# B and C of eight pairs loaded by head pair and stretch and turned on VectorE, the state of six pairs packed

## The chip, the cores and the metric

The kernel runs on one core of a Trainium2 chip. The metric is the device time of one execution in microseconds. Below, PE is TensorE (PEld its weight loads), DVE is VectorE, ACT is ScalarE, POOL is GpSimd and SP is SyncE, which here only issues DMAs.

## What is computed

A state-space scan, followed by a gated feed-forward layer without biases. There are 4 batches, 8 heads, 768 tokens, 32 channels a head (D) and 16 state rows (N). Cut to what matters:

```python
log_a = np.log(np.clip(a, 1e-06, 1.0))
for c in range(nc):                       # chunks of 32 tokens
    cum = np.cumsum(la, axis=-1)
    L = np.exp(cum[:, :, :, None] - cum[:, :, None, :]) * causal
    M = np.einsum('bhin,bhjn->bhij', Cc, Bc) * L
    y_intra = np.einsum('bhij,bhjd->bhid', M, xc)
    y_inter = np.einsum('bhin,bhnd->bhid', Cc, state) * np.exp(cum)[:, :, :, None]
    y[:, :, sl] = y_intra + y_inter
    Bx = np.einsum('bhjn,bhjd->bhjnd', Bc, xc) * np.exp(cum[:, :, -1:] - cum)[..., None, None]
    state = np.exp(np.sum(la, axis=-1))[:, :, None, None] * state + np.sum(Bx, axis=2)
x = y.transpose(0, 2, 1, 3).reshape(3072, 256)
out = (np.maximum(x @ w_gate, 0) * (x @ w_val)) @ w_out     # 256 -> 1536 -> 256
```

Inputs and output are float32. The decay from token j to token i is a product of the a between them, so a ratio of prefix products: C can be multiplied by the prefix product of its token, B by its inverse, and no decay is left between the two.

## The kernel before

**Tiling.** The scan works in chunks of 128 tokens, two chunks to a pair: 12 pairs of 256 tokens, three pairs to a batch (PPB). The feed-forward layer works in blocks of 512 tokens (two pairs): for each of 12 slices of the hidden width, gv (or gvp for 256 tokens and two slices) makes gate and val in PSUM, ACT takes the relu of gate (r), DVE multiplies by val (h). outs(b, ts) then multiplies 128 tokens of h by wo (o), ACT evacuates and SP stores.

**A pair of the scan** passes through these steps. load brings x, B and C of 256 tokens (tokens on the partitions; for pairs 4 to 11 a piece of B or C is one head's 16 values, 64 bytes). scale_bc (POOL) multiplies B and C by their decays. cast_x (POOL) makes x bf16. turn (PE, transp) transposes B and C against an identity. tevac copies C (ACT) and multiplies B twice by a 0/1 mask (DVE, for some pairs ACT), giving BT and CT with heads and state rows on the partitions. G makes C.B of each head, four row tiles of 32 partitions beside each other, into four PSUM buffers. gevac moves them to gs with the causal mask: part by DVE with maskUT, part by an ACT copy and a POOL affine_select (causal). astep adds B.x of a chunk to A_ps, all heads against all heads in one matmul of 256 columns, and sevac multiplies by smask, which keeps the blocks of equal heads (Sm, DVE). inter adds C.state to y, Dm (dterm) adds gs.x in sixteen column tiles of 32, and yevac writes yT, the feed-forward layer's input. Pairs 0 to 3 (NWIDE) are loaded two tokens to a partition and use variants (load_wide, sort_b, split_y).

**Decays.** cp is the prefix product of a along half sequences (two scans on DVE); wide_decay, decay and inverse turn it to token order through PE and keep it with its reciprocal (scaleBC).

**PSUM.** Seven buffers are shared by all steps (bank, tag "shared"), the eighth holds A_ps.

**Order.** The order of the work is written out by hand, and in_order at the end pins every engine to it: an engine executes its instructions in program order. Where pair 1 stands, for instance, POOL has weights(6, 9), cast_x(1), the masks of gevac(1, 4), weights(9, NF), and later scale(2). Around f = 8 of block 0, DVE has state(2, 0), gevac(2, 3), h of f = 8, then h of 9, 10 and 11; its neighbours on POOL are scale_bc(3), the load of wo and cast_x(3). From block 2 on a loop runs over the blocks, with the scan's steps set at fixed f.

Of the kernel before, what the change touches and what calls it, by code (L numbers as in the profile page):

```python
# [29 lines left out]
def kernel(  # L30
# [39 lines left out]


    NWIDE = 4
    st = {}

    def load_wide(p, q=nc.sync, hold=False):
        b, c0 = p // PPB, 2 * (p % PPB)
        sl = slice(c0 * 128, (c0 + 2) * 128)
        bcr = raw.tile([128, NH, 2, 2, N], FP32, tag="bcr", name="bcr")
        if hold:
            nc.vector.memset(bcr[0:1, 0, 0, 0, 0:1], 0.0)  # L80
        for src, j in ((B, 0), (C, 1)):
            q.dma_start(
                out=bcr[:, :, j].rearrange("p h r n -> p h (r n)"),
                in_=src[b, :, sl, :].rearrange("h (p r) n -> p h (r n)", r=2))
        st[p] = {"bcr": bcr}

    def load_x(p, hold=False):
# [9 lines left out]
    def load(p, q):  # L97
        b, c0 = p // PPB, 2 * (p % PPB)
        xr = raw.tile([128, 2, NH, D], FP32, tag="xr", name="xr")
        bcr = raw.tile([128, 2, 2, NH, N], FP32, tag="bcr", name="bcr")  # L100
        for i in range(2):
            sl = slice((c0 + i) * 128, (c0 + i + 1) * 128)
            q.dma_start(out=xr[:, i], in_=x[b, :, sl, :].rearrange("h s d -> s h d"))
            for src, j in ((B, 0), (C, 1)):
                q.dma_start(out=bcr[:, i, j],
                            in_=src[b, :, sl, :].rearrange("h s n -> s h n"))
# [22 lines left out]
    zero1 = const.tile([2 * BH, 1], FP32)  # L129
    nc.vector.memset(zero1, 0.0)  # L130
    tmask = const.tile([128, 2], FP32)
    nc.vector.memset(tmask, 0.0)
    smask = const.tile([128, 2, 128], BF16)
    nc.vector.memset(smask, 0.0)
# [4 lines left out]
    for q in range(4):  # L139
        r = slice(32 * q, 32 * q + 32)  # L140
        c = 64 * (q % 2)
        nc.vector.tensor_copy(
            smask[r, q // 2, c:c + 64].rearrange("p (t d) -> p t d", t=2),
            tmask[r].unsqueeze(2).to_broadcast([32, 2, 32]))
    pick = const.tile([2 * BH, 2, BH], FP32)
    pairs = identf.rearrange("p (h w) -> p w h", w=2)
    nc.vector.tensor_copy(pick[:, 1], pairs[:, 1])
# [46 lines left out]
    nc.vector.reciprocal(rmid, cp[:, H - 1:H])  # L194
    nc.vector.tensor_scalar_mul(pick[:, 0], pairs[:, 0], rmid)

    def wide_decay(ps):

        d = bank("wdec", (128, len(ps), 2, 8))
        first = True  # L200
        for k, p in enumerate(ps):
            b, c0 = p // PPB, 2 * (p % PPB)
            for i in range(2):
                w, o = (c0 + i) // HC, ((c0 + i) % HC) * 128
                for r in range(2):
                    nc.tensor.matmul(  # L206
                        out=d[64 * i:64 * i + 64, k, r],
                        lhsT=cp[:, o + r:o + 128:2], rhs=pick[:, w, 8 * b:8 * b + 8],
                        start=first or (k == 0 and r == 0), stop=True,
                        tile_position=(0, 64 * i), skip_group_check=True)  # L210
                first = False
        return d
# [53 lines left out]
    def inverse(b, c0, c1):  # L266
        nc.vector.reciprocal(scaleBC[:, b, c0:c1, 0, :], scaleBC[:, b, c0:c1, 1, :])

    yT = glob.tile([128, 2, T], BF16)
    A_ps = mm.tile([128, 2, 128], FP32, tag="Aps", name="A_ps")  # L270


    def scale(p, eng, ceng):
# [3 lines left out]
    def scale_bc(p, eng):  # L277
        b, c0 = p // PPB, 2 * (p % PPB)
        s = st[p]
        bs = att.tile([128, 4, 128], BF16, tag="bs", name="bs")  # L280
        if p < NWIDE:
            src = s["bcr"].rearrange("s h j r n -> s (j r) h n")
            f = factors[p]
        else:
            src = s["bcr"].rearrange("s i j h n -> s (i j) h n")
            f = scaleBC[:, b, c0:c0 + 2].rearrange("s c j h -> s (c j) h")
        eng.tensor_tensor(  # L287
            out=bs.rearrange("s k (h n) -> s k h n", h=NH), in0=src,
            in1=f.to_broadcast([128, 4, NH, N]), op=ALU.mult)
        if p < NWIDE:  # L290
            s["tin"] = [[bs[:, 2 * j + r] for r in range(2)] for j in range(2)]
            s["sort"] = s["tin"][0]
        else:
            s["tin"] = [[bs[:, 2 * i + j] for i in range(2)] for j in range(2)]
            s["B"] = s["tin"][0]

    def cast_x(p, ceng):
        s = st[p]
# [80 lines left out]
    def G(p):  # L379
        s = st[p]  # L380
        g = [bank("g%d" % q, (128, 2, 2, 128)) for q in range(4)]
        for i in range(2):
# [49 lines left out]
    def sevac(p, i):  # L432
        if 2 * (p % PPB) + i == NC - 1:
            return
        S[2 * p + i + 1] = n = att.tile([128, 2, 128], BF16, tag="Sm", name="Sm", bufs=5)
        nc.vector.tensor_tensor(out=n, in0=A_ps, in1=smask, op=ALU.mult)  # L436

    def state(p, i):
        astep(p, i)
        sevac(p, i)  # L440

    def y_bank(s):
        if "y" not in s:
# [33 lines left out]
    def dterm(p, out, k, i, start):  # L477

        s = st[p]
        for c in range(4):  # L480
            h = 4 * k + c
            nc.tensor.matmul(  # L482
                out=out[32 * c:32 * c + 32], lhsT=s["x"][i][:, h * D:(h + 1) * D],
                rhs=s["gs"][:, h // 2, 2 * i + h % 2], start=start, stop=True,
                tile_position=(0, 32 * c), skip_group_check=True)

    def Dm(p):
# [109 lines left out]
    def section(p, n, s=None):  # L597

        inter(p, 0)
        inter(p, 1)  # L600
        Dm(p)
        if n < NPAIR:
            G(n)
        if s is not None:
# [1 line left out]
        yevac(p, nc.scalar)  # L606
        if n < NPAIR:
            gevac(n)

    def Gs(p):  # L610
        G(p)
        gevac(p)
# [83 lines left out]
    turn(2, True)  # L696
    sort_b(2, False)
    tevac(2, nc.vector, nc.scalar)
    gv(0, 6)
    sort_evac(2)  # L700
    gv(0, 7)
    G(2)
    u = gv(0, 8, False)
    state(2, 0)
    gevac(2, 3)
    gv_evac(*u)
    scale_bc(3, nc.gpsimd)
    weights_out(0, NF)
    cast_x(3, nc.gpsimd)
    gv(0, 9)  # L710
    gv(0, 10)
# [18 lines left out]
    scale(4, nc.gpsimd, nc.gpsimd)  # L730
    gvp(1, 0, 6)
    gvp(1, 0, 8)
    inter(3, 1)
    Dm(3)
    astep(3, 1)
    yevac(3, nc.scalar)
    sevac(3, 1)
    scale(5, nc.gpsimd, nc.gpsimd)
    gvp(1, 0, 10)
    for f in range(0, 10, 2):  # L740
        gvp(1, 1, f)
    turn(4)
    tevac(4, nc.vector, nc.scalar)
    gvp(1, 1, 10)
    outs(0, 0)
    state(4, 0)
    Gs(4)
    outs(0, 1)
    state(4, 1)
    inverse(2, 0, 6)  # L750
    load(7, nc.sync)
    outs(0, 2)
    turn(5)
    tevac(5, nc.vector, nc.scalar)
    scale(6, nc.gpsimd, nc.gpsimd)
    outs(0, 3)
    load(8, nc.sync)
# [1 line left out]
    state(5, 0)  # L759
    outs(1, 0)  # L760
    inverse(3, 0, 6)
    turn(6)
    tevac(6, nc.vector, nc.scalar)
    outs(1, 1)
    outs(1, 2)
    section(5, 6)
# [2 lines left out]
    for b in range(2, NBLK):  # L769
        P, Q, R = 2 * b + 2, 2 * b + 3, 2 * b + 4  # L770
        more = P < NPAIR
        for n in (P + 3, P + 4):
            if n < NPAIR:
                load(n, nc.sync)
        fst[b] = ffn.tile([128, NF, 512], BF16, tag="h", name="h")
        for f in range(NF):
# [2 lines left out]
                continue  # L779
            if f == 0:  # L780
                scale(Q, nc.gpsimd, nc.gpsimd)
            if f == 1:
                state(P - 1, 1)
            if f == 3:
                turn(Q)
                tevac(Q, nc.vector, nc.scalar)
            if f == 4 and R < NPAIR:
                scale(R, nc.gpsimd, nc.gpsimd)
            if f == 6:
                state(P, 0)  # L790
# [45 lines left out]
```

## Time and profile before

| | |
|---|---|
| time, median of the runs | 127.63 us |
| the profiled execution: time, span | 127.66 us, 126.0 us |
| PE busy | 120.2 us, 95% of the span |
| DVE, ACT, POOL busy | 86.5, 76.9, 42.0 us |
| share of PE on the chain that ended last | 91% |
| DMA moved | 12.10 MB in 74,287 packets, 67,040 of them under 512 B |
| TensorE clock granted | 1.0 throughout |

The profile is one execution on the chip. Busy time is summed over an engine's instructions. The chain is followed back from the last instruction, at each step to what released it. A row of a timeline gives start, duration, engine, line, operation, output and inputs, count, and in brackets the idle time before it and who ended it. A row of groups gives count, busy time, mean duration in ns, then the idle time before.

### The profile page before, as it was taken

To read this page: it belongs to the slowest core of one execution; us is meant where nothing else is said; L and a number is where in the kernel's file an instruction comes from. 1 tells how busy PE (TensorE), PEld (TensorE's weight loads), DVE (VectorE), ACT (ScalarE), POOL (GpSimd) and SP (SyncE) were. 2 spreads that over 40 slices of the span, in tenths; PEclk is the share of its full clock that TensorE was granted. 3 is DMA by queue.
4 is the path that set the end of the run, shared out by engine and by line. 5 is a ranking of instruction groups with operands and counts; after the bars stand their busy time and mean duration, and the time that the engine had idled before them with its cause. 6 is when DMAs were issued, how large, how long until landed. Compare 5 with 4: busy or idle time off the path is not lost.

```text
span 126.0 us, 3223 instructions
## 1 busy us (share of the span) xinstructions
PE 120.2 (95%) x1224; PEld 82.0 (65%) x1224; DVE 86.5 (69%) x174; ACT 76.9 (61%) x153; POOL 42.0 (33%) x72
## 2 busy tenths in 40 slices
PE   6899899999999999999999999999999999999990
PEld 4578585578898988744578654588544588444770
DVE  6876978888987665579692689691798870578410
ACT  5066747979774463877863776945676634776310
POOL 7988661765405361444030660030800030000000
PEclk9999999999999999999999999999999999999999
DMA  2999999999979679989983386002200003100022
GB/s 54 197 194 180 170 153 184 140 106 165 168 90 118 106 111 158 139 181 137 119 93 78 103 104 72 5 3 83 86 5 0 0 0 128 44 0 0 0 97 70
DMA packets 74287, 12.10 MB, mean 96 GB/s; under 512 B 67040, under 2 KB 74272, under 8 KB 74272
## 3 DMA queue, kind: packets, MB, share of 16 engines
q1 hardware_dynamic: 67632, 9.02, 46.2%
q0 software_dynamic: 4272, 2.36, 14.5%
q10 hardware_dynamic: 2368, 0.52, 2.0%
q8 instruction: 9, 0.15, 0.4%
q14 instruction: 6, 0.05, 0.1%
HBM read 11.11 MB, written 3.15 MB: 113 GB/s over the span
## 4 chain that ended last, share of the span: by engine, by line
PE 91%; DMA 2%; DVE 2%; POOL 1%; ACT 1%; issue 0%
PE o L565 25%; PE gate L515 19%; PE val L518 19%; PE gate L539 6%; PE val L539 6%; PE g L386 3%; PE y L482 3%; DMA a_sb<-in_a_dram 2%; PE A_ps L428 2%; PE tp L333 2%; PE y L472 2%; POOL gs L394 1%; DVE cp L189 1%; PE w L161 1%; PE wdec L206 1%; PE dec L253 1%
## 5 line engine op out<-in xcount | busy, mean ns | idle before, releaser
L527 DVE TENSOR_TENSOR h<-r,val 128x512 bf16<-128x512 bf16 x54 | 36.5, 685 | 14.4 <-ACT r L526 13.0
L526 ACT ACTIVATE r<-gate 128x512 bf16<-128x512 f32 x54 | 31.9, 599 | 10.7 <-PE gate L515 9.1
L565 PE MATMUL o<-wo,h 128*128 128x256 bf16 x288 | 34.1, 273 | 0.0
L515 PE MATMUL gate<-yT,wg 128*128 128x512 bf16 x108 | 32.1, 379 | 0.0
L518 PE MATMUL val<-yT,wv 128*128 128x512 bf16 x108 | 32.1, 379 | 0.0
L565 PEld LDWEIGHTS <-h 128*128 128x128 bf16 x288 | 27.6, 98 | 3.9
L394 POOL TENSOR_SCALAR_AFFINE_SELECT gs<-gs 128x512 bf16<-128x512 bf16 (+1 forms) x26 | 13.5, 546 | 47.1 <-ACT gs L411 47.1
L418 DVE TENSOR_TENSOR gs<-g,maskUT 128x512 bf16<-128x512 f32 (+1 forms) x32 | 17.5, 599 | 10.0 <-issue 8.2
L518 PEld LDWEIGHTS <-wv 128*128 128x128 bf16 x108 | 10.6, 98 | 12.7
L515 PEld LDWEIGHTS <-wg 128*128 128x128 bf16 x108 | 10.2, 98 | 9.6
L554 DVE TENSOR_TENSOR h<-r,val 128x512 bf16<-128x512 bf16 x18 | 12.1, 684 | 2.1 <-ACT r L547 1.2
L411 ACT CAST gs<-g 128x512 bf16<-128x512 f32 (+1 forms) x26 | 11.8, 513 | 2.5 <-PE g L386 2.5
L547 ACT ACTIVATE r<-gate 128x512 bf16<-128x512 f32 x18 | 10.7, 602 | 4.2 <-PE gate L539 3.7
L287 POOL TENSOR_TENSOR bs<-bcr,scaleBC 128x512 bf16<-128x512 f32 x8 | 8.5, 1058 | 9.2 <-DMA bcr<-in_C_dram 5.6
L539 PE MATMUL gate<-yT,wg 128*128 128x256 bf16 x72 | 10.8, 273 | 0.0
L539 PE MATMUL val<-yT,wv 128*128 128x256 bf16 x72 | 10.8, 273 | 0.0
L579 ACT COPY ob<-o 128x256 f32<-128x256 f32 x11 | 4.1, 372 | 9.3 <-PE o L565 8.9
L436 DVE TENSOR_TENSOR Sm<-A_ps,smask 128x256 bf16<-128x256 f32 x20 | 8.3, 417 | 1.9 <-PE A_ps L428 1.7
L584 ACT COPY ob<-o 128x512 f32<-128x512 f32 x6 | 3.5, 585 | 8.0 <-PE o L565 8.0
L539 PEld LDWEIGHTS <-wv 128*128 128x128 bf16 x72 | 7.0, 98 | 0.8
L301 POOL CAST xb<-xr 128x512 bf16<-128x512 f32 x11 | 6.7, 609 | 2.6 <-DMA xr<-in_x_dram 2.6
L503 ACT CAST yT<-y 128x512 bf16<-128x512 f32 x10 | 5.9, 585 | 2.5 <-PE y L482 2.4
(86 smaller groups left out, 105.1 us busy)
## 6 DMA issues: line engine op xcount, KB each, us to landing
xr<-in_x_dram SPq DMA_DIRECT2D x24, 128.0 KB, 3.4
out_dram<-ob SPq DMA_DIRECT2D x6, 256.0 KB, 2.6
out_dram<-ob SPq DMA_DIRECT2D x10, 128.0 KB, 1.9
bcr<-in_B_dram SPq DMA_DIRECT2D x16, 64.0 KB, 3.2
bcr<-in_C_dram SPq DMA_DIRECT2D x16, 64.0 KB, 3.0
wo<-in_moe_w_out_dram POOLq DMA_DIRECT2D x1, 768.0 KB, 8.8
bcr<-in_B_dram SPq DMA_DIRECT2D x3, 128.0 KB, 4.8
wg<-in_moe_w_gate_dram POOLq DMA_DIRECT2D x3, 128.0 KB, 4.8
```

Source lines behind the costliest of these rows:

```text
L287: eng.tensor_tensor(out=bs.rearrange("s k (h n) -> s k h n", h=NH), in0=src, in1=f.to_broadcast([128, 4, NH, N]), op=ALU.mult)
L394: nc.gpsimd.affine_select(out=dst, in_=dst, pattern=[[0, n], [1, 128]], compare_op=ALU.is_ge, fill=0.0, base=0, channel_multiplier=-1)
L411: nc.scalar.copy(out=d[:, q, h], in_=g[q][:, h])
L418: nc.vector.tensor_tensor(out=d[:, q, h], in0=g[q][:, h], in1=m[:, h], op=ALU.mult)
L515: nc.tensor.matmul(out=g, lhsT=wg[:, k, fs], rhs=yT[:, k, tk], start=(k == 0), stop=(k == 1))
L518: nc.tensor.matmul(out=v, lhsT=wv[:, k, fs], rhs=yT[:, k, tk], start=(k == 0), stop=(k == 1))
L526: nc.scalar.activation(r, g, AF.Relu)
L527: nc.vector.tensor_tensor(out=fst[b][:, f], in0=r, in1=v, op=ALU.mult)
L539: nc.tensor.matmul(out=o[:, j], lhsT=w[:, k, fs], rhs=yT[:, k, tk], start=(k == 0), stop=(k == 1), skip_group_check=True)
L547: nc.scalar.activation(r, g, AF.Relu)
L554: nc.vector.tensor_tensor(out=fst[b][:, f:f + 2, u * 256:(u + 1) * 256], in0=r, in1=v, op=ALU.mult)
L565: nc.tensor.matmul(out=o[:, ts % 2], lhsT=fst[b][:, f, ts * 128:(ts + 1) * 128], rhs=wo[:, f], start=(f == 0), stop=(f == NF - 1), skip_gr ...
```

## The change

For batches 1 to 3 (except pair 3's own wide load) B and C are also loaded a whole batch at a time (load_seq): partition 32q + j holds stretch j of 24 tokens of the heads q and q + 4, so a contiguous piece is 24 x 16 values, 1,536 bytes. Their decays are made in the same layout: a is loaded so (load_a), one DVE scan gives the products inside all stretches, the stretch totals are turned, scanned and turned back (seq_decay) and multiplied in on POOL. seq_scale (POOL, 768 elements a partition) applies them; seq_turn (DVE) transposes 32x32 blocks, which gives heads and state rows on the partitions and the batch's 768 tokens along them; seq_mask (POOL) makes the two masked copies of B. G takes its slices from there. The transposes on PE, their evacuation, and the token-order load of C go for pairs 4 to 11; B is still loaded in token order too, for the state. Heads are paired q with q + 4 from batch 1 on.

For pairs 6 to 11 (NRUN on) the state is made by arun in the section that precedes the pair: column tiles of 32, only for blocks of paired heads, into a part of the A_ps buffer, with both states of a pair evacuated by one DVE product against a wider smask.

In the order: smask_seq (eight small POOL copies) and three memsets stand behind cast_x(1); load_a behind load_x(2); load_seq(1) ahead of load(4) and load_seq(2) ahead of load(6); the local scan behind gv(0, 6), seq_decay behind h of f = 8; seq_scale(1, "B") ahead of G(3) and its masks; the turns of batch 1 between the gvp of block 1 and behind outs(0, 0), those of batch 2 behind outs(0, 2), those of batch 3 in block 2. Gs(4) moves behind outs(0, 1).

```diff
 def load(p, q):
...
-            for src, j in ((B, 0), (C, 1)):
-                q.dma_start(out=bcr[:, i, j],
-                            in_=src[b, :, sl, :].rearrange("h s n -> s h n"))
+            q.dma_start(out=br[:, i], in_=B[b, :, sl, :].rearrange("h s n -> s h n"))
+    def load_seq(b, q):
+        for src, k in ((B, "B"), (C, "C")):
+            r = raw.tile([128, 2, U, N], FP32, tag="seq" + k, name="seq" + k, bufs=2)
+            q.dma_start(out=r.rearrange("p t u n -> p t (u n)"),
+                in_=src[b].rearrange("(t q) (j u) n -> (q j) t (u n)", t=2, u=U))
...
+    def smask_seq():
+        for q in range(4):
+            r = slice(32 * q, 32 * q + 32)
+            for v in range(1, 3):
+                nc.gpsimd.tensor_copy(smasks[r, v, :, 32 * q:32 * q + 32],
+                    tmask[r].unsqueeze(2).to_broadcast([32, 2, 32]))
...
+    def seq_decay():
+        for k in range(2):
+            nc.vector.tensor_tensor_scan(
+                out=lead[:, k, 1:17], data0=tott[:, 16 * k:16 * k + 16],
+                data1=zero.to_broadcast([128, 16]), initial=1.0, op0=ALU.mult, op1=ALU.add)
+        nc.vector.reciprocal(half, lead[:, 0, 16:17])
+        nc.vector.tensor_scalar_mul(mids[:, 0:16], lead[:, 0, 0:16], half)
+        nc.vector.tensor_copy(mids[:, 16:32], lead[:, 1, 0:16])
+        nc.vector.transpose(out=pre, in_=mids)
+    def seq_scale(b, k):
+        nc.gpsimd.tensor_tensor(
+            out=o.rearrange("p u (t n) -> p t u n", t=2), in0=r,
+            in1=f.unsqueeze(3).to_broadcast([128, 2, U, N]), op=ALU.mult)
+    def seq_turn(b, k, lo, hi):
+        nc.vector.transpose(
+            out=s[k + "T"].rearrange("p (j u) -> p u j", u=U)[:, lo:hi], in_=o[:, lo:hi])
+    def seq_mask(b):
+        for t in range(2):
+            nc.gpsimd.tensor_scalar_mul(m[:, t], s["BT"], tmask[:, t:t + 1])
...
+    def arun(p):
+        c0 = 2 * (p % PPB)
+        for c in range(max(c0 - 2, 0), c0 + 1):
+            v0, v1 = (0 if c < c0 else 1), (1 if c == c0 - 2 else 2)
+            for q in range(4):
+                nc.tensor.matmul(
+                    out=XY[32 * q:32 * q + 32, v0:v1], lhsT=st[pc]["B"][i][:, 32 * q:32 * q + 32],
+                    rhs=rhs.unsqueeze(1).to_broadcast([128, v1 - v0, 2, 32]), ...
...
     cast_x(1, nc.gpsimd)
+    smask_seq()
+    for v in (a0, tot, lead):
+        nc.gpsimd.memset(v, 0.0 if v is a0 else 1.0)
     gvp(0, 0, 0)
...
-    for n in (4, 5, 6):
-        load(n, nc.sync)
+    load_seq(1, nc.sync)
+    load(4, nc.sync)
+    load(5, nc.sync)
+    load_seq(2, nc.sync)
+    load(6, nc.sync)
...
     gv_evac(*u)
+    seq_decay()
     scale_bc(3, nc.gpsimd)
     weights_out(0, NF)
+    nc.gpsimd.tensor_tensor(out=local, in0=local, in1=pre..., op=ALU.mult)
     cast_x(3, nc.gpsimd)
...
-    inverse(1, 2, 6)
+    seq_inverse(1)
+    seq_scale(1, "B")
     gvp(1, 0, 2)
     G(3)
+    inverse(1, 2, 6)
...
-    turn(4)
-    tevac(4, nc.vector, nc.scalar)
...
     section(p, n):   Dm(p); arun(n) for n >= NRUN; G(n); yevac(p); gevac(n); the state's product
```

More of the change, by code (lines that the diff above doesn't have):

```diff
@@ L435, in sevac @@
         S[2 * p + i + 1] = n = att.tile([128, 2, 128], BF16, tag="Sm", name="Sm", bufs=5)
-        nc.vector.tensor_tensor(out=n, in0=A_ps, in1=smask, op=ALU.mult)
+        nc.vector.tensor_tensor(out=n, in0=A_ps, in1=smasks[:, min(p // PPB, 1)],
+                                op=ALU.mult)
     def state(p, i):
@@ L608, in section @@
             gevac(n)
+        if more:
+            evac()
     def Gs(p):
@@ L737 @@
     sevac(3, 1)
+    scale(4, nc.gpsimd, nc.gpsimd)
     scale(5, nc.gpsimd, nc.gpsimd)
     gvp(1, 0, 10)
-    for f in range(0, 10, 2):
+    for f in range(0, 12, 2):
         gvp(1, 1, f)
-    turn(4)
-    tevac(4, nc.vector, nc.scalar)
-    gvp(1, 1, 10)
+    seq_inverse(2)
+    seq_scale(2, "B")
     outs(0, 0)
+    seq_turn(1, "C", 0, 12)
+    seq_turn(1, "C", 12, U)
+    seq_scale(2, "C")
     state(4, 0)
+    outs(0, 1)
     Gs(4)
-    outs(0, 1)
     state(4, 1)
@@ L752 @@
     outs(0, 2)
-    turn(5)
-    tevac(5, nc.vector, nc.scalar)
+    for k in "BC":
+        seq_turn(2, k, 0, 12)
+        seq_turn(2, k, 12, U)
+    seq_mask(2)
     scale(6, nc.gpsimd, nc.gpsimd)
```

175 lines of the change are left out of this document (135 added, 40 removed).

## The prediction

> **What bounds the kernel now.** I read the page first (busy shares, slices, chain), then the windows, then the timelines of single stretches.
>
> ```profile
> span 126.0 us, 3223 instructions
> PE 120.2 (95%) x1224; PEld 82.0 (65%) x1224; DVE 86.5 (69%) x174; ACT 76.9 (61%) x153; POOL 42.0 (33%) x72
> PE 91%; DMA 2%; DVE 2%; POOL 1%; ACT 1%; issue 0%
> core 0: us, PE busy (x) PEld busy (x) DVE busy (x) ACT busy (x) POOL busy (x), PEclk, DMA share, GB/s
> 10.00:17.00 7.00, 6.50 (x96) 4.92 (x94) 5.79 (x12) 4.20 (x9) 5.35 (x8) 1.00 1.30 176
> 17.00:22.00 5.00, 5.00 (x56) 3.58 (x54) 4.21 (x10) 3.60 (x7) 1.65 (x2) 1.00 1.13 165
> 22.00:27.00 5.00, 5.00 (x60) 2.79 (x49) 4.11 (x8) 4.32 (x10) 4.10 (x6) 1.00 0.95 129
> 27.00:32.00 5.00, 5.00 (x67) 4.16 (x68) 4.43 (x9) 4.47 (x10) 1.72 (x4) 1.00 1.40 151
> ```
>
> PE is the bound: 91% of the chain, and in the windows from 17 us on its busy time equals the window. So two things alone move the end: PE work that goes away, and PE waits that appear. PE has no gap left in which a new wait could hide. The same rows show where one is near: from 22 to 32 us DVE is busy 8.54 of 10 us, and from 10 to 17 us POOL is busy 5.35 of 7. The profiled execution took 127.66 us, 1.66 more than its span; the median of the runs is 127.63, so I add 1.66 to a span and compare with that median.
>
> **PE work removed: the transposes.** Pairs 4 to 11 lose four each, 32 in all. Price, from start to start:
>
> ```profile
> 37.59 0.39 PE L333 MATMUL tp<-ident,bs 128*128 128x128 bf16 x4
> 37.82 0.60 PE L539 MATMUL gate<-yT,wg 128*128 128x256 bf16 x4
> ```
>
> The four hold PE from 37.59 to 37.82, 0.23 us. Eight times that is 1.8 us, all on the path. Their evacuations on ACT and DVE go too, but those engines do not set the end here.
>
> **PE work exchanged: the state.** Pairs 6 to 11 lose ten A_ps matmuls, and get 56 column-tiled ones (per batch 4 + 12 + 12) of 64 or 128 columns.
>
> ```profile
> 72.38 0.27 PE L428 MATMUL A_ps<-xb,bs 128*128 128x256 bf16 x1
> 72.49 0.59 PE L515 MATMUL gate<-yT,wg 128*128 128x512 bf16 x2
> 25.11 0.41 PE L482 MATMUL y<-gs,xb 128*32 128x128 bf16 x16
> 25.45 0.60 PE L515 MATMUL gate<-yT,wg 128*128 128x512 bf16 x2
> L482 PE MATMUL y<-gs,xb 128*32 128x128 bf16 x192 | 5.1, 222 | 0.5 <-DVE gs L418 0.3 <-POOL gs L394 0.2
> ```
>
> One A_ps step holds PE 0.11 us (72.38 to 72.49), ten 1.1. The new matmuls have the form of the y group and stand right behind it, so no change of tiling is added. Sixteen of those take 0.41 in all, 0.222 each, so their starts lie 0.19/15 = 12.5 ns apart; 56 of them are 0.7 us. Net gain 0.4. Ends: 64 columns pass faster, so 0.35 for all 56 is possible (gain 0.75); at the 0.34 us per sixteen that the y group holds PE (25.11 to its successor at 25.45, drain included) they cost 1.2 (loss 0.1). I take the spacing.
> The Trainium skill, "TensorEngine Tiling (Array Packing)", section Instruction Overhead, speaks against this part: about 60 cycles a matmul however short. At 2.4 GHz 56 of them would be an estimated 1.4 us, a loss of 0.3 instead of the gain, and the sum below would be 0.7 higher. The 12.5 ns row contradicts the rule for concurrent column tiles, at least at 128 columns.
>
> So PE has 2.2 us less to do, 1.5 to 2.6 by the ends.
>
> **Added wait A: small POOL work ahead of pair 1's mask.** smask_seq (eight copies of 32 x 64 elements) and three memsets (128 x 144, 32 and 34 f32) are put behind cast_x(1), ahead of gevac(1, 4).
>
> ```profile
> 13.31 0.60 POOL L301 CAST xb<-xr 128x512 bf16<-128x512 f32 x1 [1.16 <-DMA xr<-in_x_dram]
> 14.22 1.22 POOL L394 TENSOR_SCALAR_AFFINE_SELECT gs<-gs 128x512 bf16<-128x512 bf16 x2 [0.31 <-ACT gs L411]
> 15.50 0.29 PE L482 MATMUL y<-gs,xb 128*32 128x128 bf16 x6 [0.17 <-POOL gs L394]
> 0.34 0.10 POOL L820 MEMSET const-float32-1.0<- 128x1 f32 x1
> 0.38 0.10 POOL L820 MEMSET const-bfloat16-1.0<- 128x1 bf16 x1
> 0.80 0.14 POOL masks.py:197 MEMSET identf<- 64x64 f32 x1 [0.29 <-POOLq L820]
> 2.79 0.60 POOL L154 COPY order<-ident 128x128 bf16<-128x128 bf16 x2
> 3.32 0.89 POOL L174 DMA_DIRECT2D wg<-in_moe_w_gate_dram  x1
> ```
>
> POOL casts x(1) until 13.91, idles 0.31, and masks gs from 14.22 to 15.44; PE takes up split_y(1) at 15.50 having waited 0.17 for exactly that. This is on the chain: what POOL does more than 0.31 us of here, PE waits for. Two 128-element copies hold POOL 0.53 us (2.79 to 3.32), 0.265 each; 64 elements lie between half that (0.13) and that. I take 0.18, eight 1.45; the memsets about 0.35, by the 0.14 us of 64 elements. That is 1.8, less 0.31: **1.5 us**. Far ends: a spacing of 0.04, as between the one-element memsets (0.34 to 0.38), gives about 0.2 net; 0.3 and more for each copy 2.5. Queued behind the masks on POOL are the loads of the weights of blocks 9 to 11, which pair 0 and 1's block uses last, so those cost nothing.
>
> **Added wait B: seq_decay on DVE among the h products.** After h of f = 8, DVE gets two scans of 16, a reciprocal, a product, a copy and a 32x32 turn; behind it stand h of 9, 10 and 11, which give back the PSUM buffers of val.
>
> ```profile
> 24.54 1.87 DVE L527 TENSOR_TENSOR h<-r,val 128x512 bf16<-128x512 bf16 x3
> 26.77 0.60 PE L539 MATMUL gate<-yT,wg 128*128 128x256 bf16 x4
> L189 DVE TENSOR_TENSOR_SCAN cp<-a_sb,zero 64x256 f32<-64x256 f32 x1 | 0.7, 683 | 0.3 <-DMA a_sb<-in_a_dram 0.3
> L189 DVE TENSOR_TENSOR_SCAN cp<-a_sb,cp,zero 64x128 f32<-64x128 f32 x1 | 0.5, 476 | 0.0
> L194 DVE RECIPROCAL rmid<-cp 64x1 f32<-64x1 f32 x1 | 0.2, 155 | 0.0
> L195 DVE TENSOR_SCALAR pick<-identf,rmid 64x32 f32<-64x32 f32 x1 | 0.2, 232 | 0.0
> L243 DVE COPY wf<-wdec 128x16 f32<-128x16 f32 x1 | 0.1, 110 | 0.0
> ```
>
> Two scan lengths give 1.6 ns an element and 0.27 at length zero, so 0.3 a scan; 0.16, 0.23 and 0.11 for the next three, and 0.2 assumed for the turn, which no row shows (0.1 by the copy, 0.5 by the scan). Sum 1.3, with starts overlapping about 1.15. Seven buffers go round in the order in which they are given back; by that order (worked out from the code; the rows do not name banks) the gate of gvp(1, 0, 0) at 26.77 takes the val of f = 10, free at 24.54 + 1.87 = 26.41. Cover 0.36; **wait 0.8 us**. Ends: 0 if another buffer is free, 1.7 if the turn is dear or the small steps wait on POOL. The scan of 144 (0.5) and two small steps before h of 7 and gs(2) fit into DVE's idle time there.
> The Trainium skill, "SBUF — State Buffer", section Who interferes with whom, has a rule against this place: a DVE instruction with two SBUF inputs and a POOL one that reads SBUF lock each other out. The scans have two, and scale_bc(3) is then on POOL; by the rule wait B would be an estimated 0.3 us longer. No row shows such a scan beside POOL.
>
> **Other edits.** POOL gets seq_scale(1, "B") ahead of pair 3's masks:
>
> ```profile
> 29.76 1.58 POOL L394 TENSOR_SCALAR_AFFINE_SELECT gs<-gs 128x512 bf16<-128x512 bf16 x3 [2.61 <-ACT gs L411]
> 31.89 0.41 PE L482 MATMUL y<-gs,xb 128*32 128x128 bf16 x16
> L287 POOL TENSOR_TENSOR bs<-bcr,scaleBC 128x512 bf16<-128x512 f32 x8 | 8.5, 1058 | 9.2 <-DMA bcr<-in_C_dram 5.6 <-DVE h L554 2.0 <-PE tp L333 1.5
> ```
>
> At 1.058 us for 512 elements, 768 take 1.6. seq_inverse, behind wait B, frees it near 30.0; masks 31.6 to 33.2, the first two done at 32.6; pair 3's y matmuls come at 31.89 + 0.8 = 32.7. So 0 to 0.5, I take 0.15. On DVE the twelve turns (384 elements; 0.4 to 0.7 each, an estimate from the 0.62 us an h product of 512 takes in the row of three) and six wider state products replace six BT products and ten Sm products. Most of the turns stand between 38 and 52 us:
>
> ```profile
> 38.00:44.00 6.00, 6.00 (x71) 5.16 (x70) 4.60 (x9) 2.71 (x6) 2.71 (x5) 1.00 0.81 110
> 44.00:52.00 8.00, 8.00 (x131) 6.78 (x130) 4.25 (x9) 4.48 (x11) 2.50 (x5) 1.00 0.91 141
> ```
>
> DVE is busy 8.85 of these 14 us and POOL 5.21, so they have room, and pair 4's G stands one outs later. The wider smask memset eats 0.27 us of DVE idle before the first scan: nothing. Loads: C of eight pairs in 64-byte pieces (16,384 packets) goes, 1,536 packets of 1,536 bytes come; SP issues 16 DMAs fewer of C and 6 more for whole batches, two more for pair 3 and one for a. I cost them at nothing while they land in time (second rival).
>
> **Sum**: -1.8 - 0.4 + 1.5 + 0.8 + 0.15 = +0.25. Span 126.25, time **127.9 us**, no change to speak of; 2% (125.1 and 130.2) is about what a measurement of this kernel can tell from no change.
>
> **Rivals.**
> First, the waits are mostly covered: POOL pipelines its small copies as it does the one-element memsets (A 0.2 to 0.6) and a free buffer covers B. Then -2.2 + 0.6 gives 126.0. For it: the 0.04 spacing. Against: 0.265 for a copy of only 128 elements. Over 2% faster needs all 2.6 us of gain and no wait.
>
> Second, slower: the whole-batch load holds POOL's queue. seq_scale(1, "B") needs 393 KB of B; pair 3's masks stand behind it, and PE's y(3) behind them.
>
> ```profile
> 21.48 1.40 SPq L103 DMA_DIRECT2D xr<-in_x_dram  x1
> 25.44 1.08 POOL L178 DMA_DIRECT2D wo<-in_moe_w_out_dram  x1
> L105 SPq DMA_DIRECT2D bcr<-in_C_dram x1: 661/661/661, 25.9 to 25.9; - x1
> DMA to landing us min/median/max: 7.3/7.3/7.3
> ```
>
> The load stands where xr(4) is issued, 21.48, behind two more DMAs, so near 22.5; a 64 KB load that ran beside wo took 7.3 us. At 5 us it lands at 27.5 and hides. The point is 30.0: each microsecond later is one of PE. If it goes out at 24.5 and takes 8, it lands at 32.5: +2.5, 130.4 us.
>
> Third, the packed state gains nothing and the turns leave DVE behind: matmul price at the 0.34 end (+0.5) and B at 1.7 (+0.9) give 129.3.
>
> That the transposes do not go isn't a rival: the code no longer has them.
>
> **How the numbers follow.** Forecast 0.54 (126.7 to 129.0); first rival 0.22 (125.2 to 126.7, of which 0.05 with still less waiting lies below 125.1); second 0.17 (129.3 to 132); third 0.07. The forecast's own range by its ends is 126.7 to 129.0. For 8 in 10 I take in most of the first rival, the third and the lower half of the second: 125.7 to 130.6. Faster by over 2%: 0.05; slower: 0.2; within: 0.75.
>
> **What would show it.** Transposes: 16 tp matmuls left of 48 (both banks), PE busy down by about 2 us. State: the new groups behind y hold PE 0.05, 0.15 and 0.15 us. A: in pair 1's stage the first mask starts 1.5 us later behind eight copies, and PE waits for "POOL gs" about 1.7 instead of 0.17. B: a PE gap of about 0.8 before gvp(1, 0, 0), released by DVE h. Second rival: POOL idle ahead of its 768-element product with the release from a DMA. I am wrong if small POOL copies cost far from 0.18, if PE stalls between 38 and 52 us on masks, or if the span falls by the full 2.2.

## The result and the profile after

The changed kernel took 141.56 us (median of six executions, 140.78 to 144.49) against 127.63. The ratio is 1.110, interval 1.106 to 1.115. Some executions of either kernel take several per cent longer than the rest; a median counts them, a ratio and its interval leave them out. The profiled execution took 140.78 us at a span of 139.1, so again about 1.7 us lie around the span. The forecast was 127.9, and its range ended at 130.6: **the loss of 13.9 us lies outside it**.

The head of the page and its chain of work, after:

```profile
span 139.1 us, 3265 instructions
PE 122.6 (88%) x1232; PEld 81.7 (59%) x1238; DVE 105.8 (76%) x188; ACT 73.0 (53%) x141; POOL 64.0 (46%) x106
PE 58%; DVE 15%; POOL 11%; issue 7%; DMA 6%; ACT 1%; SPq 0%; DVEq 0%; POOLq 0%
```

PE held 91% of the chain before; now DVE and POOL hold 26% together. DVE is busy 19.3 us longer and POOL 22.0. The windows of the stretch in which eight of the twelve turns stand, after (columns as before: length, then busy time of PE, PEld, DVE, ACT, POOL, then the granted clock):

```profile
38.00:44.00 6.00, 5.29 (x49) 4.60 (x48) 6.00 (x10) 3.58 (x6) 3.51 (x2) 1.00 0.93 194
44.00:52.00 8.00, 5.71 (x66) 4.67 (x65) 7.69 (x12) 1.45 (x3) 7.34 (x11) 1.00 0.43 74
52.00:58.00 6.00, 5.19 (x76) 4.29 (x73) 6.00 (x4) 2.88 (x6) 2.72 (x2) 1.00 0.84 135
58.00:62.00 4.00, 0.65 (x15) 0.41 (x19) 2.82 (x6) 0.00 (x0) 3.91 (x6) 1.00 0.34 104
62.00:66.00 4.00, 3.95 (x41) 2.59 (x42) 1.95 (x4) 1.78 (x4) 2.36 (x6) 0.57 0.02 4
```

Before, DVE was busy 8.85 of the 14 us from 38 to 52, and PE all of them. Now DVE is busy 13.69 of these 14 us and all of the next 6, and PE loses time in the first four rows and runs on a lower clock in the last. The groups by line say with what DVE and POOL are full:

```profile
L349 DVE STREAM_TRANSPOSE BTs<-pad 128x384 bf16<-128x384 bf16 x6 | 11.3, 1951 | 0.0
L349 DVE STREAM_TRANSPOSE CTs<-pad 128x384 bf16<-128x384 bf16 x6 | 11.2, 2055 | 0.0
L357 POOL TENSOR_SCALAR BM<-BTs,tmask 128x768 bf16<-128x768 bf16 x6 | 13.2, 2204 | 8.3 <-DVE BTs L349 8.3
```

A turn takes 2.0 us, where the prediction had 0.4 to 0.7. All twelve take 22.5 us, not 6.6 (12 x 0.55). The masked copies of B on POOL, to which the prediction gave no price, take 13.2. The waits of PE, after:

```profile
PE y L603 <- DVE Sm L536: 3.3, 1, 3.3
PE y L613 <- POOL gs L494: 2.2, 3, 1.1
PE A_ps L528 <- POOL xb L396: 1.3, 1, 1.3
PE g L486 <- DVE CTs L349: 1.0, 1, 1.0
```

The largest one can be read in the timelines of DVE (first three rows) and PE (the others) around it:

```profile
51.53 3.64 DVE L349 STREAM_TRANSPOSE BTs<-pad 128x384 bf16<-128x384 bf16 x2
54.80 3.90 DVE L349 STREAM_TRANSPOSE CTs<-pad 128x384 bf16<-128x384 bf16 x2
58.32 1.82 DVE L518 TENSOR_TENSOR gs<-g,maskUT 128x512 bf16<-128x512 f32 x3
60.53 0.29 PE L603 MATMUL y<-CTs,Sm 128*128 128x128 bf16 x2 [3.33 <-DVE Sm L536]
62.85 2.74 PE L697 MATMUL o<-wo,h 128*128 128x256 bf16 x12
```

Batch 2's four turns hold DVE from 51.53 to 58.7. Behind them stand gs of pair 5 and then Sm(5, 0), which PE needs at 57.2 and gets at 60.5. Then the granted clock is 0.57, and the twelve o matmuls take 2.74 us (1.48 before).

Where the time is lost, by the starts of the same PE work in the two timelines:

| PE work | before | after | later by |
|---|---|---|---|
| gate of gvp(0, 1, 0), behind wait A | 16.85 | 18.53 | 1.7 |
| gate of gvp(1, 0, 0), behind wait B | 26.77 | 30.28 | 3.5 |
| outs(0, 0) | 38.69 | 43.47 | 4.8 |
| inter of section(4, 5) | 44.81 | 51.88 | 7.1 |
| inter of section(5, 6) | 50.08 | 56.92 | 6.8 |
| block 2 | 52.39 | 65.39 | 13.0 |

From there to the end nothing more is lost: the span is 13.1 longer. So all of it stands ahead of block 2, 9.5 of it behind wait B, where the turns and masks are. Of these 9.5, PE is idle for 7.2 between 38 and 62 us (first four rows of the windows), the clock of 0.57 behind them costs an estimated 1.7 (4 us x 0.43), and about 0.5 stand at pair 3's y, whose masks on POOL come late.

### The profile page after: what moved, and what is told of

Read it like the earlier page. It is cut to its first block, busy times and chain, and to the rows that moved or that the text cites. A ratio compares the mean times of both kernels' runs of the same rounds, so it can differ in the third digit from the quotient of the medians.

```text
span 139.1 us, 3265 instructions
## 1 busy us (share of the span) xinstructions
PE 122.6 (88%) x1232; PEld 81.7 (59%) x1238; DVE 105.8 (76%) x188; ACT 73.0 (53%) x141; POOL 64.0 (46%) x106
## 3 DMA queue, kind: packets, MB, share of 16 engines
q0 software_dynamic: 4272, 2.36, 13.2%
## 4 chain that ended last, share of the span: by engine, by line
PE 58%; DVE 15%; POOL 11%; issue 7%; DMA 6%; ACT 1%; SPq 0%; DVEq 0%; POOLq 0%
PE val L650 17%; PE gate L647 16%; PE o L697 14%; DMA xr<-in_x_dram 3%; DVE CTs L349 3%; POOL gs L494 3%; DVE BTs L349 3%; DVE h L686 3%; PE gate L671 3%; PE val L671 2%; POOL pad L339 2%; DMA a_sb<-in_a_dram 2%; PE y L613 2%; POOL BM L357 2%; PE g L486 2%
## 5 line engine op out<-in xcount | busy, mean ns | idle before, releaser
L658 ACT ACTIVATE r<-gate 128x512 bf16<-128x512 f32 x54 | 32.2, 598 | 12.7 <-PE gate L647 11.9
L697 PE MATMUL o<-wo,h 128*128 128x256 bf16 x288 | 34.7, 279 | 0.7 <-DVE h L659 0.7
L697 PEld LDWEIGHTS <-h 128*128 128x128 bf16 x288 | 28.1, 100 | 5.9 <-issue 1.4
L647 PE MATMUL gate<-yT,wg 128*128 128x512 bf16 x102 | 30.9, 380 | 0.0
L518 DVE TENSOR_TENSOR gs<-g,maskUT 128x512 bf16<-128x512 f32 (+1 forms) x32 | 18.1, 617 | 6.4 <-issue 5.2
L650 PEld LDWEIGHTS <-wv 128*128 128x128 bf16 x108 | 10.6, 98 | 13.1 <-issue 0.5
L357 POOL TENSOR_SCALAR BM<-BTs,tmask 128x768 bf16<-128x768 bf16 x6 | 13.2, 2204 | 8.3 <-DVE BTs L349 8.3
L671 PE MATMUL gate<-yT,wg 128*128 128x256 bf16 x72 | 11.7, 288 | 0.4 <-DVE h L659 0.4
L671 PE MATMUL val<-yT,wv 128*128 128x256 bf16 x72 | 11.3, 281 | 0.7 <-DVE h L686 0.7
L349 DVE STREAM_TRANSPOSE BTs<-pad 128x384 bf16<-128x384 bf16 x6 | 11.3, 1951 | 0.0
L349 DVE STREAM_TRANSPOSE CTs<-pad 128x384 bf16<-128x384 bf16 x6 | 11.2, 2055 | 0.0
L716 ACT COPY ob<-o 128x512 f32<-128x512 f32 x6 | 3.5, 586 | 13.9 <-PE o L697 13.9
```

Source lines behind the costliest of these rows:

```text
L349: nc.vector.transpose(out=s[k + "T"].rearrange("p (j u) -> p u j", u=U)[:, lo:hi], in_=o[:, lo:hi])
L357: nc.gpsimd.tensor_scalar_mul(m[:, t], s["BT"], tmask[:, t:t + 1])
L518: nc.vector.tensor_tensor(out=d[:, q, h], in0=g[q][:, h], in1=m[:, h], op=ALU.mult)
L647: nc.tensor.matmul(out=g, lhsT=wg[:, k, fs], rhs=yT[:, k, tk], start=(k == 0), stop=(k == 1))
L650: nc.tensor.matmul(out=v, lhsT=wv[:, k, fs], rhs=yT[:, k, tk], start=(k == 0), stop=(k == 1))
L658: nc.scalar.activation(r, g, AF.Relu)
```

## Experiments

My theory after this profile ("turns"): the twelve turns are slow because they write each element 48 bytes from the last (the 24 tokens of a stretch lie beside each other in the output), and as DVE is full from 30 to 58 us their time comes out at the end. Rivals: POOL's 2.2 us masks, wait A with the clock behind it, and a turn that is dear in whatever layout.

**What a turn costs: forms and steps.** In forms, B's turn writes whole blocks, and C's two turns become one of 768 elements with the same step as before:

```diff
-            out=s[k + "T"].rearrange("p (j u) -> p u j", u=U)[:, lo:hi], in_=o[:, lo:hi])
+            out=s["BT"].rearrange("p (u j) -> p u j", u=U)[:, lo:hi], in_=o[:, lo:hi])  # B
+            out=s["CT"].rearrange("p (j u) -> p u j", u=U), in_=o)                      # C, once
```

> What makes a turn cost 1.95 to 2.05 us for 384 elements. Here B is turned into block order (each 32x32 block is written densely, two instructions of 384 as before), C with the same 48-byte step as in the change but in one instruction of 768. The tokens of B come out permuted and the decays of the whole-batch copies are left out (a in their place), so that the numbers stay small. Theory 'step': the strided write is dear, so B's turns fall to about 0.5 us and C's one turn takes about 4. Rival 'block': 0.16 us for each of the 12 blocks however it is written; B stays at 1.95, C about 3.9. Rival 'instruction': a fixed cost each time; B stays at 1.95, C takes about 2.5.

The groups of forms:

```profile
L353 DVE STREAM_TRANSPOSE CTs<-pad 128x768 bf16<-128x768 bf16 x3 | 11.0, 3660 | 0.0
L350 DVE STREAM_TRANSPOSE BTs<-pad 128x384 bf16<-128x384 bf16 x6 | 3.2, 554 | 0.0
```

Same data, same count of blocks: 0.55 us written whole, 1.95 with the step. That is theory 'step'; one instruction in the place of two saves little (3.66 against 3.90 for C's two in a row shown above). So the cost is in the step of the write. The time, 134.57 us, is of a single execution, in which four gate matmuls near 14 us took 1.06 us in the place of 0.60, so it is only a rough one.

In steps, each turn groups its blocks so that neighbours of a block land r elements apart:

```diff
+        r = {(1, "B"): (1, 2), (1, "C"): (3, 4), (2, "B"): (6, 12), (2, "C"): (0, 0),
+             (3, "B"): (2, 3), (3, "C"): (4, 6)}[b, k][lo > 0]
...
+            out = s[k + "T"][:, 32 * lo:32 * hi].rearrange("p (g j r) -> p g r j", j=32, r=r)
```

> How a turn's cost follows the step of its write. All turns have 384 elements a partition (12 blocks of 32x32); the columns of a block are written 1, 2, 3, 4, 6 or 12 elements of two bytes apart, in batch 2 C as in the change 24 apart; the tokens come out permuted, and the decays of the whole-batch copies are left out. Theory 'any step': a dense write packs columns and any other does not, so step 1 takes 0.55 us and every step from 2 on 1.8 to 2.0. Theory 'far step': the cost grows with the bytes between columns (0.6 at 4 bytes, 1.0 at 12, 1.95 from 24 or 48 on). If 2 to 4 elements are cheap, a load in pieces of 2 to 4 tokens can keep the token order.

DVE's timeline of steps, turn by turn, for r = 1, 2, 3, 4, 6 and 12:

```profile
36.77 0.57 DVE L362 STREAM_TRANSPOSE BTs<-pad 128x384 bf16<-128x384 bf16 x1
72.21 0.60 DVE L362 STREAM_TRANSPOSE BTs<-pad 128x384 bf16<-128x384 bf16 x1
44.12 0.77 DVE L362 STREAM_TRANSPOSE CTs<-pad 128x384 bf16<-128x384 bf16 x1
76.72 1.01 DVE L362 STREAM_TRANSPOSE CTs<-pad 128x384 bf16<-128x384 bf16 x1
48.51 1.42 DVE L362 STREAM_TRANSPOSE BTs<-pad 128x384 bf16<-128x384 bf16 x1
49.65 2.00 DVE L362 STREAM_TRANSPOSE BTs<-pad 128x384 bf16<-128x384 bf16 x1
```

A step of 2 bytes costs 0.57 us, 4 bytes 0.60, 6 bytes 0.77 (0.81 in a second turn), 8 bytes 1.01, 12 bytes 1.42 (1.49) and 24 bytes 2.00; the 48 bytes of the change took 2.13 in the same execution. So the cost is nearly flat up to 4 bytes, grows with the distance from there to 24, and hardly rises between 24 and 48. That is theory 'far step', only that 12 bytes cost more than its 1.0.
The Trainium skill, "VectorE: DVE Perf Modes", section The three transpose paths, gives 311 ns for a turn of 128x128 bf16 on VectorE. Our 384 elements are three of those, an estimated 0.93 us: more than the 0.55 to 0.60 measured for near writes, and less than half of the 1.95 that this kernel's write costs. For this turn that section names no dependence on how the output is written.

**Is that the loss? copies, masks_dve, late.** In copies, each turn becomes a plain DVE copy of the same 384 elements, everything else queued as it was:

```diff
-        nc.vector.transpose(
-            out=s[k + "T"].rearrange("p (j u) -> p u j", u=U)[:, lo:hi], in_=o[:, lo:hi])
+        nc.vector.tensor_copy(
+            s[k + "T"].rearrange("p (u j) -> p u j", u=U)[:, lo:hi], o[:, lo:hi])
```

> The twelve turns are replaced by DVE copies of the same tiles with dense writes (about 0.2 us each), so B and C are not turned and, as above, their decays are left out; every instruction and wait behind a turn stays in its place. Theory 'turns': the 22 us of turns are the larger part of the loss of 13.9; the waits that end in a turn or in a product queued behind one in the changed kernel's profile (0.7, 1.0 and 3.3 us of PE) and most of the half clock after 60 us go, the span falls by 6 to 8, time 134 to 135.5. Rival 'masks': POOL's masks (6 of 2.2 us) and what is queued behind them set it, turns only share; then 138 to 140.

It took 129.94 us (median of four; ratio 1.014, 1.006 to 1.022), where I had expected 134 to 135.5. Besides the turns it leaves out the decays of the whole-batch copies. The groups and the largest wait of PE in copies:

```profile
L349 DVE COPY CTs<-pad 128x384 bf16<-128x384 bf16 x6 | 2.0, 376 | 0.0
L349 DVE COPY BTs<-pad 128x384 bf16<-128x384 bf16 x6 | 1.7, 294 | 0.0
PE y L613 <- POOL gs L494: 2.8, 3, 1.4
```

With 3.7 us of copies in place of 22.5 us of turns, the waits for Sm(5, 0), x of pair 4 and CTs are gone. The two ratios differ by 0.096 (1.110 less 1.014), about **12 of the 13.9 us**. Not all of that is the turns'. The two profiles differ by 11.9 us. Of these, 1.7 stand ahead of the first turn (gate of gvp(1, 0, 0) at 28.61 in copies, at 30.28 in after), mostly because the clock stayed full there, as shown under late. About 0.5 more lie at pair 3's y, where POOL has no decays to wait for in copies. Some 9.7 us are left for the turns with the slow clock from 62 to 66 us that follows their waits. I had booked part of that to POOL's masks and to the clock; but POOL was late mostly because the turns that feed it were. What the masks cost without the turns is the last row: POOL holds its two masks of batch 2 from 46.71 to 51.20, and PE then waits 1.4 us for pair 5's gs.

In masks_dve the two masked copies go to DVE (`nc.vector.tensor_scalar_mul` for `nc.gpsimd...` in seq_mask).

> The six masked copies of B move from POOL (2.2 us each) to DVE (bf16 from SBUF to SBUF; 0.3 to 0.5 us each expected); turns as in the change. Theory 'turns': POOL's queue gets 13 us shorter, pair 4's state no longer waits for x (1.3) nor pair 5's y for its masks (0.8), but DVE keeps the turns: 138 to 140. Rival 'masks': 133 to 135.

142.06 us in the median of four, ratio 1.097 (1.090 to 1.104), so 140.0 by the ratio: the upper end of theory 'turns'. The groups, the longest wait of PE and the gate behind wait B:

```profile
L357 DVE TENSOR_SCALAR BM<-BTs,tmask 128x768 bf16<-128x768 bf16 x6 | 2.7, 484 | 0.0
PE y L603 <- DVE Sm L536: 3.9, 1, 3.9
28.62 0.60 PE L671 MATMUL gate<-yT,wg 128*128 128x256 bf16 x4 [0.40 <-DVE h L659]
```

The same copy is 484 ns on DVE, 2204 on POOL. But taking all 13.2 us from POOL gains only about 1.7 us by the ratios. In the profile that much is won before any mask runs: the gate stands at 28.62 instead of 30.28, with the full clock from 17 to 22 us. Behind it 2.7 us more stand in DVE's full queue, Sm(5, 0) comes 3.9 us late instead of 3.3, and the span is only 0.4 us shorter than that of after. The masks by themselves are not the cause.

In late, smask_seq and the memsets move from in front of pair 1's masks to behind scale(2) on POOL.

> The eight small POOL copies and the three memsets stand behind the scaling of pair 2 instead of ahead of pair 1's masks. Theory 'A with clock': wait A was 1.7 us (gate of block 0's second half at 18.53 instead of 16.85), and the halved clock that follows it until 21.2 another 1.2; both go: 138.3 to 139 (2.6 to 3.2 less). Rival 'A alone': the low clock has another cause and stays, 139.6 to 140. Rival 'absorbed': the later waits for turns and loads take up what is gained, 141.

138.92 us, ratio 1.086 (1.080 to 1.091), in the expected range: the gate behind wait A starts at 16.98 instead of 18.53. Of the gain of 3.1 us by the ratios, 1.5 stand in that gate. In the profiles another 1.2 follow at once: from this gate to that of gvp(1, 0, 0) pass 11.75 us in after and 10.53 in late (to 27.51). That is the clock: from 17 to 22 us it averaged 0.66 in after and 1.00 in late. But in copies, which has wait A as well, it was 1.00 too, and the same stretch took 10.52:

```profile
17.00:22.00 5.00, 5.00 (x48) 3.89 (x48) 2.54 (x8) 1.57 (x3) 3.11 (x6) 0.66 1.07 145
17.00:22.00 5.00, 5.00 (x63) 4.05 (x58) 3.93 (x10) 2.73 (x6) 3.01 (x6) 1.00 1.06 144
```

(first row after, second row copies). masks_dve, with wait A, has 1.00 there as well. So the slow clock can follow wait A but need not, and what decides it stays open; the time fell in the range of 'A with clock', but only the 1.5 us are shown to come from moving the copies.

**All three taken away: cml, and the packed state: cml_norun.** cml is copies, masks_dve and late in one; cml_norun is cml with the state of pairs 6 to 11 made as before (`NRUN = NPAIR`, and the state steps back at their places).

> Turns replaced by dense DVE copies (B and C are not turned, their decays left out), the masked copies of B on DVE, the small POOL work behind pair 2's scaling: the change with its three dear terms taken away, all dependencies kept. By the forecast's own terms the wait of 1.24 us at pair 1 goes from the 128.9 of the run with copies alone, and up to 1 us of waits for POOL's masks: 126.5 to 127.5, equal to the kernel before or a little under. Rival: what was gained comes back at the loads of batch 1 and 2 or at DVE between 22 and 32 us: 128 to 129.

> As cml, with the state of pairs 6 to 11 as before the change (ten matmuls of 256 columns and ten products, no column tiles). By the forecast's term the packed state is worth 0.4 us of PE, by the changed kernel's trace 0.6 (twelve tiles lengthen the step from y to G from 0.34 to 0.45 us, four to 0.37): 0.3 to 0.7 slower than cml. Rival 'the tiles gain nothing': equal within 0.2 or faster.

cml took 126.23 us, ratio 0.988 (0.986 to 0.990), a little below the expected range; cml_norun 127.43, ratio 0.995 (0.992 to 0.998). So with the turns, the decays, POOL's masks and wait A away, the rest of the change gains 1.2% of the time before, and the packed state is 0.7% of it (0.2 to 1.2 by the intervals), some 0.9 us, a little more than the 0.3 to 0.7 expected. The engines of cml's and then of cml_norun's page:

```profile
PE 117.7 (94%) x1238; PEld 79.7 (64%) x1238; DVE 91.5 (73%) x194; ACT 72.9 (58%) x141; POOL 51.4 (41%) x100
PE 118.6 (94%) x1192; PEld 80.2 (64%) x1192; DVE 91.0 (72%) x198; ACT 72.9 (58%) x141; POOL 51.3 (41%) x100
```

PE is busy 2.5 us less than the 120.2 of before; 0.9 of that is the state, 1.6 the transposes. One wait of PE over 0.5 us is in cml that the kernel before does not have. POOL (first row) and DVE around it, and that wait:

```profile
20.88 1.76 POOL L171 CAST smasks<-tmask 32x64 bf16<-32x64 f32 x8
23.10 0.85 DVE L848 TENSOR_TENSOR_SCAN hd<-ah,a 128x144 f32<-128x144 f32 x1 [1.37 <-POOL ah L844]
PE gate L647 <- DVE h L659: 2.0, 1, 2.0
```

The place to which late moved the small copies is no good one: DVE's scan now waits for POOL behind them, the h products wait behind the scan, and PE waits 2.0 us for h. The profiled execution took 127.24 us, above the median, so the wait may be shorter in others.

**Can it be had whole? best_dve, best_act, best2.** These leave nothing out. The turn writes whole blocks, and the passes that follow put the tokens in order as they read; the small copies stand behind pair 3's x, where they hold up neither the masks nor the scan.

```diff
+            out=s["raw"][k].rearrange("p (u j) -> p u j", u=U)[:, lo:hi], in_=o[:, lo:hi])
...
+            nc.vector.tensor_copy(s["CT"].rearrange("p (j u) -> p j u", u=U),
+                                  s["raw"]["C"].rearrange("p (u j) -> p j u", u=U))
...
-            nc.gpsimd.tensor_scalar_mul(m[:, t], s["BT"], tmask[:, t:t + 1])
+            nc.vector.tensor_scalar_mul(m[:, t].rearrange("p (j u) -> p j u", u=U),
+                s["raw"]["B"].rearrange("p (u j) -> p j u", u=U), tmask[:, t:t + 1])
```

> Nothing is left out. Each turn writes its blocks whole (0.55 us for 384 elements, as in the run forms), and what puts the tokens in order is a copy: both masked copies of B read the turned tile with a step of 32 elements, on DVE, and C gets one such copy on DVE. The 3x2 masks leave POOL. The small masks of the packed state stand behind pair 3's x on POOL, so that neither pair 1's diagonal masks nor the local scan wait for them. Per pair of batches DVE then has 4 x 0.56 + 3 passes of 768 elements. A dense mask of 768 took 0.48 (masks_dve); if the stepped read loses that, I take 0.9 (the 512-element products from fp32 take 0.69), so 2.2 + 2.7 = 4.9 us a batch instead of 7.9, against 1.3 + 1.0 = 2.3 in the run that had copies, DVE masks and late small masks and took 126.23. Theory 'DVE is full from 30 to 58 us and the turns' time comes straight out of the end': of the 2 x 2.6 = 5.2 us added to that run in this stretch, what exceeds DVE's idle time there counts, 0 to 4; less up to 1.4 for the scan that no longer waits behind the small masks: 125.5 to 129.5, most likely 127.5. Rival 'a stepped read costs as much as a stepped write' (about 2 us for 384, so 4 for 768): 3 x 4 + 2.2 = 14 us a batch, over 138.

> As best_dve, but one masked copy of B and the copy of C on ACT (0.9 to 1.1 us each, estimated from its 512-element copies). DVE then has 4 x 0.56 + 0.9 = 3.1 us a batch, 0.8 more than in the run that took 126.23. Theory 'DVE is the bound of that stretch': below best_dve by 0.5 to 2, 125 to 127.5, most likely 126. Rival 'ACT's relu and evacuations for PE are hit by its two passes instead': equal to best_dve or up to 2 above it.

The groups of best_dve, then those of best_act for what it gives to ACT, and its largest wait of PE:

```profile
L364 DVE TENSOR_SCALAR BM<-BTr,tmask 128x768 bf16<-128x768 bf16 x6 | 5.8, 1009 | 0.0
L352 DVE STREAM_TRANSPOSE BTr<-pad 128x384 bf16<-128x384 bf16 x6 | 3.2, 554 | 0.0
L355 DVE COPY CTs<-CTr 128x768 bf16<-128x768 bf16 x3 | 3.0, 1001 | 0.1
L364 ACT ACTIVATE BM<-BTr,tmask 128x768 bf16<-128x768 bf16 x3 | 4.8, 1597 | 2.2 <-DVE BTr L352 2.2
L355 ACT COPY CTs<-CTr 128x768 bf16<-128x768 bf16 x3 | 4.5, 1496 | 5.3 <-DVE CTr L352 5.3
PE gate L680 <- ACT yT L644: 2.4, 1, 2.4
```

best_dve took 129.22 us, ratio 1.011 (1.008 to 1.015), inside its range at the slow side: a stepped read costs twice a dense one (1.01 against 0.48 us), so DVE does 15.0 us of this work (the rows shown and 3.0 for C's turns) in the place of 22.5, with POOL's 13.2 gone. With the small copies moved as well, that wins back 12.6 us by the ratios, 3.0 of them (in the profiles) ahead of the gate of gvp(1, 0, 0), and still no gain against before is left. best_act took 134.5, ratio 1.049 (1.043 to 1.055): there neither range held. The rival had the right kind of loss, too small. Its passes took 1.5 to 1.6 us, not 0.9 to 1.1, and as ACT stands idle for DVE's turn ahead of them (5.3 and 2.2 us in the rows), yT and gs behind them are late: PE waits 2.4 us for ACT's yT.

best2 spreads best_dve's passes: batch 1's C into the products before outs(0, 0), and batch 2's ordering copy to ACT and one mask behind state(5, 0).

> best_dve with its passes put where DVE and ACT have room: C of batch 1 turned and put in order inside the six products before outs(0,0) (there its first consumer waited 1.4 us for it at 42.7), of batch 2 the ordering copy of C on ACT and one of the masks behind state(5,0), so that Sm(5,0) no longer queues behind them (1.1 us of wait at 52.4). B of batch 2 is scaled while POOL is idle (38.9 to 41.8). Nothing is left out. Theory 'what is left of the loss is the two waits of best_dve': 2.5 us below its 129.2, so 126.5 to 127.2. Rival 'DVE is full from 30 to 54, so work moved forward comes out of the h products that PE waits for': 128 to 129.5, with the waits now at the val and gate products of the loop.

128.48 us (13 executions), ratio 1.006 (1.004 to 1.008): the rival's time. The profiled execution took 130.57 us, so only its waits are read, and those with care: Sm(5, 0) no longer delays PE there, but PE waits 0.9 us for CTs and 1.4 for an earlier Sm between 42 and 46 us. These are not the val and gate products that the rival named, so its reason is not shown.

No whole version that I ran beats the kernel before; only cml and, by 0.5%, cml_norun are below it, and both leave the ordering and the decays out.

## Why the prediction was wrong, step by step

- **The step that failed is the term of the turns**, "384 elements; 0.4 to 0.7 each", and the cover drawn from it ("they have room"). I priced an operation that no row showed by an h product, gave it only a narrow band and put nothing on the far end. Written whole, the turn is in that band (0.55); written as the diff writes it, 1.95 to 2.06. Twelve are 22.5 us instead of 6.6, eight of them in or next to a stretch where DVE had some 5 us free of 14. By copies that is about 10 us of the 13.9; its whole difference of 12 has in it a clock that stayed full and decays left out.
- **A second step that failed in that place**: seq_mask on POOL got no price at all, and takes 6 x 2.2 us. Two masks stand ahead of x of pair 4, for which PE waits 1.3 us in after, and without the turns PE waits 1.4 us behind them (copies). While the turns stand, moving the masks gains nothing that shows (masks_dve). Copies to cml takes them away together with wait A, and gains 3.3 us by the ratios (1.014 to 0.988).
- **Transposes, -1.8**: right; 16 of 48 are left, and cml_norun shows PE busy 1.6 less. (After itself shows 122.6, 2.4 more than before, as matmuls on the slow clock last longer: 2.74 us for twelve above, in the place of 1.48.)
- **State, -0.4**: right in sign, somewhat small. The profile has twelve packed matmuls between y and G in one section of after and four in another:

```profile
75.99 0.41 PE L613 MATMUL y<-gs,xb 128*32 128x128 bf16 x16
76.44 0.40 PE L486 MATMUL g<-CTs,BM 32*128 32x128 bf16 x16
95.69 0.41 PE L613 MATMUL y<-gs,xb 128*32 128x128 bf16 x16
96.06 0.40 PE L486 MATMUL g<-CTs,BM 32*128 32x128 bf16 x16
```

  From y to G pass 0.45 and 0.37 us; without them y holds PE for 0.34 (25.11 to 25.45 in the prediction's rows). Twelve cost 0.11, four 0.03, all 56 about 0.5 against 1.1 for what goes: -0.6, and the two runs show -0.9. The 60 cycles a matmul of the Trainium skill, "TensorEngine Tiling (Array Packing)", section Instruction Overhead, don't add up for these column tiles: 9 ns each in the row, against the prediction's 25 (1.4 us for 56). As the tiles' matmuls overlap (0.222 us each, starts 12.5 ns apart), neither the 9 nor the 12.5 ns shows what one alone costs, so "contradicts the rule" was too strong. The low end of 1.5 us for all of PE's gain came from that estimate; by the rows alone it is 1.7.
- **Wait A, +1.5**: right. The eight copies and three memsets hold POOL from 13.42 to 15.66. Where the clock stayed full (copies), the gate started at 18.09, 1.24 later than before; in after it was 1.7. The first rival's cheap copies (0.2 to 0.6) are refuted. What I had not counted is the slow clock that followed in the profile of after.

```profile
13.42 1.77 POOL L171 CAST smasks<-tmask 32x64 bf16<-32x64 f32 x8
15.66 1.22 POOL L494 TENSOR_SCALAR_AFFINE_SELECT gs<-gs 128x512 bf16<-128x512 bf16 x2
```

- **Wait B, +0.8**: there, released by DVE's h as said, but 0.4, and two errors partly cancel. The small steps took 1.53 us (28.05 to 29.58), not 1.15: scan and turn cost what was assumed (0.29 on average and 0.21), but the product and the copy of 16 elements took 0.70 and 0.57. Against that, the gate at 30.28 follows the first of the three h products behind them (29.58 to 30.23), not the second, h of f = 10, so the buffer that PE waited for was not the one the prediction worked out.

```profile
28.05 0.50 DVE L320 TENSOR_TENSOR_SCAN lead<-tott,zero 128x16 f32<-128x16 f32 x2
29.58 1.84 DVE L659 TENSOR_TENSOR h<-r,val 128x512 bf16<-128x512 bf16 x3
30.28 0.60 PE L671 MATMUL gate<-yT,wg 128*128 128x256 bf16 x4 [0.41 <-DVE h L659]
```

- **Pair 3's masks, +0.15**: about 0.5, the end of the range given. From the gate of gvp(1, 0, 0) to the A_ps step behind pair 3's y pass 6.09 us in after, 5.59 in copies.
- **Second rival, a late load**: wrong as to the cause. Ahead of its first 768-element product POOL waited 2.3 us for DVE's reciprocal of the decays, not for the DMA.
- **First rival, no waits (126.0)**: wrong, as A and B are both there. Take wait A out of the forecast and 126.4 is left, next to cml's 126.23; but that agreement is partly luck. In cml's profile PE is busy 2.5 us less, not 2.2, wait B and the wait of pair 3's masks are gone, and the 2.0 us wait behind the moved copies stands in their place.
- **Third rival, the packed state gains nothing (129.3)**: wrong; the state gained, and B was 0.4, not 1.7.

## What to carry to other kernels

Work taken from a full engine is paid where it lands: ask of each new instruction not only how many elements it has but how far apart it writes and reads them, and if no row of the profile shows that form, give its price both ends and see what the far end does to the queue behind it. An engine with a third of its time free has no room for a block of 7 us in front of a small product that PE needs next; count what stands behind it. And a rearrangement that looks free as an access pattern may have to be paid in another pass: here it cost 1.4 us in each turn, or 0.5 in each masked copy of B and a whole pass of 1.0 for C.

## What the hardware showed that I had not expected

- A DVE 32x32 turn of 384 bf16 elements a partition: 0.54 to 0.60 us for writes 2 or 4 bytes apart, 0.77 to 0.81 at 6, 1.01 at 8, 1.42 to 1.49 at 12, 2.00 at 24, 1.95 to 2.13 at 48.
- The product of 768 bf16 elements with a scalar of the partition: 0.48 us on DVE, 0.85 to 1.01 there with a stepped read (best_act, best_dve), 1.60 on ACT with that read, 2.2 on POOL.
- Small DVE steps beside POOL's issue of the wo load took 0.70 and 0.57 us in after, and both ended when that issue ended, at 29.42; in copies, late and best_dve they end with it too. In cml, where POOL's issue had ended at 26.79, they took 0.24 and 0.17. The first scan of 16 took 0.41 in after, beside POOL's product of scale_bc(3), and 0.18 in cml. The rows are after's (first three) and cml's:

```profile
28.70 0.70 DVE L324 TENSOR_SCALAR mids<-lead,half 128x16 f32<-128x16 f32 x1
28.84 0.57 DVE L325 COPY mids<-lead 128x16 f32<-128x16 f32 x1
28.35 1.07 POOL L208 DMA_DIRECT2D wo<-in_moe_w_out_dram  x1
27.28 0.24 DVE L324 TENSOR_SCALAR mids<-lead,half 128x16 f32<-128x16 f32 x1
```
